# One chip core, three chained layers: TensorE's order fixed from the third group on, and another order of the start

## The chip, the core and the metric

The kernel runs on one NeuronCore of a Trainium2 chip, as one launch. The metric is device time in microseconds, the median of several executions. The core's engines work side by side, each through its own queue in order: TensorE (PE in the rows; PEld is its weight loads) multiplies matrices into PSUM, VectorE (DVE) and ScalarE (ACT) read PSUM and do elementwise work, GpSimd (POOL) does small jobs and indirect transfers, and SyncE (SP) issues the loads.

## The reference

Three layers follow each other on 4 x 768 = 3072 tokens of 384 numbers (8 heads of 48): a gated linear attention, a gated MLP with RMS norm, and a mixture of 8 experts with one expert per token.

```
for t in range(S):
    state = alpha[:, :, t, :, None] * state + np.einsum('bhd,bhe->bhde', k[:, :, t], v[:, :, t])
    y[:, :, t] = np.einsum('bhd,bhde->bhe', q[:, :, t], state)
...
xn = x / sqrt(mean(x*x) + 1e-6) * rms_g
x2 = (silu(xn @ w_gate) * (xn @ w_val)) @ w_out
...
e = argmax(x2 @ r_gate);  h = maximum(x2 @ w1[e], 0)
out = gate_w * sigmoid(x2 @ r_ogate)[e] * (h @ w2[e])
```

All inputs and outputs are 32-bit floats. The kernel splits each operand of the large products into a high and a low part and adds three products (high x high, high x low, low x high).

## The kernel before

**Tiles and groups.** The tokens are cut into 24 tiles of 128 tokens, numbered from 0; three tiles make a group of 384 tokens, and there are 8 groups. A tile's attention has a prework (alpha, q and k turned so that features lie on partitions, two scans along the tokens, two multiplies; `prework`, `prework_nat`) and five stages (`stages`): the score `ps_s` (line 416: 8 matmuls, two per head pair, that use rows 0 to 47 and 64 to 111 and write two banks), a transpose of the keys `ps_k` (L436), the output `ps_y` (L447 with the running state in the tile `wide`, L451 with the masked scores P), the new state `ps_st` (L472), and the transpose of the normed tile `ps_x` (L493). For tiles below `NAT` = 5 the prework turns the operands on TensorE from a buffer `nat` (L270); for tiles up to `PET` - 1 it does so from `row_a`, `row_k`, `row_q` (L371), three groups of four transposes per tile; from tile `PET` on, VectorE turns them (L376) out of block buffers `blk_a`, `blk_k`, `blk_q`, which take four loads each (L250).

**The MLP.** A group goes through 12 steps j, each of three slots: gate `ps_g` and value `ps_v` (9 matmuls each of 128 x 384, `mm3`, L595) and, one step later, the output `ps_o` (9 matmuls, `m_out`, L629). Between value and output stand a multiply on VectorE (`tt`, L606), a copy on ScalarE (`hh`, L609) and a subtraction on VectorE (`hl`, L615). The first two groups run in four pieces, s = 0 to 3 (groups 0 and 1 with the first six steps of the weights, then with the last six), since the weights arrive as 64-bit numbers and are converted on VectorE meanwhile (`conv_step`, L515 to L531). From s = 4 on (group 2), one piece is one group. `due` says in which slots the attention's stages of tiles 3 to 8 are written, a condition in the loop over g does the same for the later ones. Behind group 7 come the experts.

**The order.** The program is written in this order, and a scheduler then orders each engine's instructions by its own estimate of when each can start. `tc.keep_in_program_order(ins)` pins an instruction to the order of the source. Before the change, that is done for the warm-up matmuls (`warm`, L805, into the bank `junk`) and for instructions of VectorE, ScalarE and GpSimd whose kind stands in the list in force (`pace`; `K0` for the start, `K1` for s = 0, `K2` later). No attention or MLP matmul is pinned. The start, the attention of tiles 0 to 2 and the first loads, is written out by hand in two strings, `START` and `LOADS`: a, r, k, q are pieces of a tile's prework, s, n, y, d, x its stages, c three conversion steps, w6 six warm-up matmuls.

```python
def pace(kind, ins):
    if kind in paced[0] or kind.rstrip('0123456789') in paced[0]:
        tc.keep_in_program_order(ins)
```

Of the kernel before, what the change touches and what calls it, by code (L numbers as in the profile page):

```python
# [17 lines left out]
OFF = bass.IndirectOffsetOnAxis  # L18

CFG = {  # L20
    'START': 'a0 r0 c a1 w6 q0 k0 k1 r1 q1 w0 s0 s0 a2 y0 s1 r2 c q2 y0 w0 s1 x0 k2 y1 w4 y1 x1 s2 s2 y2 y2 x2 n1 n0 c n2 l l x2 d1 d0 c d2 w0 x0 x1 d2 d1 d0',
    'LOADS': 'a0 q0 a1 k0 q1 k1 a2 v0 w g k2 v1 q2 w w w r w v2 w w w w',
    'SEATS': (3, 5, 4, 6, 1, 1, 0, 5, 0, 2, 4, 4, 5, 3, 3, 2, 6, 1, 4, 4, 4, 2, 2, 1, 6, 3, 0, 6, 6, 4),
# [6 lines left out]
    'AHEAD': 0,  # L30
    'PREP6': 9,
    'CR': [3, 4, 3, 4],
    'PRN': [1, 2, 1, 2],
    'JS': 6,
    'ABUF': 1,
    'ZBUF': 1,
    'IB': 0,
    'RA0': 2,
    'RB0': 13,
    'XG': 3,  # L40
    'TS': 3,
    'RA': 7,
    'RB': 9,
    'LEADG': 6,
    'NAT': 5,
    'PET': 8,
    'NO': 'arkq',
}

# [3 lines left out]
def gla_glu_moe_kernel(  # L53
# [16 lines left out]
    nc = tc.nc  # L70
    P = 128
# [132 lines left out]
    xT = {}  # L204
    SEATS = CFG['SEATS']
    spread = [True]
    junk = [psM.tile([P, 4, P], F32, tag='o2', name='junk')]
    paced = [CFG['K0']]

# [191 lines left out]
    def stages(t):  # L401
        b, c = place_of[t]
        first, final = c == 0, c == NCH - 1
        en, qT, kT = pre[t]
        Sc = state_of[b % BS]
        S_ = wide[0]
        rs = [slice(64 * hh, 64 * hh + D) for hh in range(2)]
        g, ti = divmod(t, GT)
        Pt = {}

        def score():
            ps = [bank([P, NP, P], "ps_s") for _ in range(2)]
            for p in range(NP):
                for hh in range(2):
                    r = slice(64 * hh, 64 * hh + D)
                    nc.tensor.matmul(ps[hh][:, p, :], lhsT=kT[r, p, :], rhs=qT[r, p, :], start=True, stop=True)  # L416

            def post():
                if not first:
                    nc.vector.tensor_tensor(out=Sc, in0=Sc, in1=en.to_broadcast([P, NP, D]), op=ALU.mult)  # L420
                    for hh in range(2):
                        nc.scalar.activation(S_[rs[hh], :, hh * D:hh * D + D], Sc[rs[hh]], AF.Copy)
                mb = mask.to_broadcast([P, NP, P])
                for hh in range(2):
                    Ph = seat_of(t, f"P{hh}", [P, NP, P])
                    pace(f'Ph{t}', nc.vector.tensor_tensor(out=Ph, in0=ps[hh], in1=mb, op=ALU.mult))
                    Pt[hh] = Ph
            return post
        yield score

        def ktr():
            if final:
                return None
            ps = bank([P, NP, P], "ps_k")
            for p in range(NP):
                nc.tensor.transpose(ps[:, p, :], kT[:, p, :], ident)  # L436
            kn = seat_of(t, "kn", [P, H, 64])
            nc.scalar.activation(kn, ps.rearrange("p a (h d) -> p (a h) d", h=2), AF.Copy)
            Pt["kn"] = kn
            return None  # L440
        yield ktr

        def outp():
            ps = bank([P, DM], "ps_y")
            if not first:
                for p in range(NP):
                    nc.tensor.matmul(ps[:, p * 2 * D:p * 2 * D + 2 * D], lhsT=qT[:, p, :], rhs=S_[:, p, :],  # L447
                                     start=(p == 0), stop=False, skip_group_check=True)
            for h in (0, 2, 4, 6, 1, 3, 5, 7):
                for u in (slice(0, 64), slice(64, P)):  # L450
                    nc.tensor.matmul(ps[u, h * D:h * D + D], lhsT=Pt[h % 2][:, h // 2, u], rhs=vt[t][:, h, :],  # L451
                                     start=first, stop=True, skip_group_check=True)

            def post():
                xn = seat_of(t, "xn", [P, DM])
                ss = att.tile([P, 1], F32, tag="ss", name="ss", bufs=2)
                pace(f'xs{t}', nc.scalar.activation(xn, ps, AF.Square, accum_out=ss))  # L457
                nc.gpsimd.tensor_scalar(out=ss, in0=ss, scalar1=1.0 / DM, scalar2=1e-6, op0=ALU.mult, op1=ALU.add)  # L458
                pace(f'ss{t}', nc.gpsimd.tensor_tensor(out=ss, in0=ss, in1=mhalf, op=ALU.pow))
                pace(f'xa{t}', nc.scalar.activation(xn, ps, AF.Copy, scale=ss[:, 0:1]))  # L460
                Pt["xn"] = xn
            return post
        yield outp

        def state():
            if final:
                return None
            kn = Pt["kn"]
            ps = bank([P, NP, D], "ps_st")
            for p in range(NP):  # L470
                for hh in range(2):
                    nc.tensor.matmul(ps[64 * hh:64 * hh + 64, p, :], lhsT=kn[:, 2 * p + hh, :],  # L472
                                     rhs=vt[t][:, 2 * p + hh, :], start=True, stop=True)

            def post():
                if first:
                    nc.scalar.activation(Sc, ps, AF.Copy)
                else:
                    nc.vector.tensor_tensor(out=Sc, in0=ps, in1=Sc, op=ALU.add)
            return post  # L480
        yield state

        def xtr():
            if t and t + 2 < NTILE:
                load_v(t + 2)
            if ti == 0:
                xT[g] = (act.tile([P, KD, G], F32R, tag="xh", name="xh"),
                         act.tile([P, KD, G], F32R, tag="xl", name="xl"))
            xh, xl = xT[g]
            xn = Pt["xn"]  # L490
            ps = bank([P, KD, P], "ps_x")
            for kc in range(KD):
                nc.tensor.transpose(ps[:, kc, :], xn[:, kc * P:kc * P + P], ident)  # L493
            sl = slice(ti * P, ti * P + P)

            def post():
                xf = xn.rearrange("p (a b) -> p a b", a=KD)
                for kc in range(KD):
                    pace(f'xg{t}', nc.scalar.activation(xf[:, kc, :], ps[:, kc, :], AF.Copy, scale=gT[:, kc:kc + 1]))
                pace(f'xh{t}', nc.scalar.activation(xh[:, :, sl], xf, AF.Copy))  # L500
                pace(f'xl{t}', nc.vector.tensor_tensor(out=xl[:, :, sl], in0=xf, in1=f(xh[:, :, sl]), op=ALU.subtract))
            return post
        yield xtr
# [87 lines left out]
    def mm3(ps, wh, wl, xh, xl):  # L591
        n = 0
        for kc in range(KD):
            for a_, b_ in ((wh, xh), (wh, xl), (wl, xh)):
                nc.tensor.matmul(ps, lhsT=a_[:, kc, :], rhs=b_[:, kc, :],  # L595
                                 start=(n == 0), stop=(n == 3 * KD - 1))
                n += 1

    def m_val(g, j):
# [21 lines left out]
    def m_out(s, j):  # L621
# [4 lines left out]
        for i in range(GT):  # L626
            sl = slice(i * P, i * P + P)
            for n, (a_, b_) in enumerate(((hh, "woh"), (hh, "wol"), (hl, "woh"))):
                nc.tensor.matmul(obank[s][i], lhsT=a_[:, sl], rhs=weight(b_, j),  # L629
                                 start=(j == j0 and n == 0), stop=(j == j1 - 1 and n == 2))  # L630

    rows = {}

# [55 lines left out]
    def route_b(g):  # L689
        oh, ohb, ohc, m8, og, se = rt.pop(g)  # L690
        R = rows[g]
        ps = psR[0].tile([P, GT + 1, E], F32, tag=psR[1], name="ps_r")
        nc.tensor.matmul(ps[:, 0:1, :], lhsT=tri_b, rhs=ohb[:, 0:1, :], start=True, stop=True)
        for i in range(1, GT):
            nc.tensor.matmul(ps[:, i, :], lhsT=tri_b, rhs=ohb[:, i, :], start=True, stop=False)
            nc.tensor.matmul(ps[:, i, :], lhsT=ones_b, rhs=ohc[:, i - 1, :], start=False, stop=True)
        nc.tensor.matmul(ps[:, GT, :], lhsT=ones_b, rhs=ohc[:, GT - 1, :], start=True, stop=True)
        bc = [P, GT, E]

        nc.vector.tensor_scalar(out=se, in0=se, scalar1=1e-9, scalar2=2.0, op0=ALU.add, op1=ALU.mult)  # L700
# [151 lines left out]
    def due(s, n):  # L852
# [1 line left out]
        if s == 0:  # L854
            return done < GS and (n + 1 - AHEAD) * GS >= (done + 1) * (N - AHEAD - CFG['TS'])
        k_ = done - GS
        return (n + 1 + N * (s - 2)) * GS >= (k_ + 1) * 2 * N and k_ < GS and (k_ < NST - 1 or s >= CFG['XG'])

    for s in range(4):
        N = 3 * (runs[s][2] - runs[s][1])  # L860
        paced[0] = CFG['K2'] if s else CFG['K1']
        for n in range(N):
# [193 lines left out]

    for g in range(2, NG):
        last = g == NG - 1
        if last:
            psA.release()  # L1060
            att.release()
# [285 lines left out]
```

## Time and profile before

| | before |
|---|---|
| median of 3 runs | 876.1 us (875.66 to 876.71) |
| profiled execution | 880.26 us, span 878.6 us |
| TensorE busy | 856.1 us, 97% |
| VectorE / ScalarE / GpSimd busy | 489.3 / 326.0 / 143.8 us |
| chain that ended last | TensorE 85%, DMA 5%, issue 4% |
| mean granted TensorE clock | 0.99 |

Times in the profile are of one execution, which lies 4.2 us above the median; its span is counted from the first to the last instruction. Matmuls overlap, so their durations add up to more than the time they take: what one costs is read from one start to the next. A matmul of 32-bit floats (not of the kind fp32r that the wide ones use) shows as two rows, so a score of 8 shows as x16.

### The profile page before, as it was taken

What the parts mean: (1) busy time and instruction counts of PE and PEld (TensorE: products, weight loads), DVE (VectorE), ACT (ScalarE), POOL (GpSimd) and SP (SyncE); (2) the same over time, 40 slices, a digit from 0 to 9 for tenths busy, and PEclk for the clock granted to TensorE, in tenths of its full rate; (3) what the DMA queues carried; (4) which work ended last, traced back from release to release, by engine and by line L of the source; (5) the groups of instructions that cost most, each with busy time, mean ns of one, the idle gap of its engine ahead of it and who ended that gap; (6) DMA issues with size and microseconds to landing.
All of it is one profiled execution on the core that took longest, in us unless ns stands there. A gap on an engine that the chain in (4) does not pass through costs nothing.

```text
span 878.6 us, 15655 instructions
## 1 busy us (share of the span) xinstructions
PE 856.1 (97%) x6042; PEld 814.5 (93%) x6042; DVE 489.3 (56%) x1108; ACT 326.0 (37%) x708; POOL 143.8 (16%) x204
## 2 busy tenths in 40 slices
PE   7999999999999999999999999999999999999994
PEld 6799999899999999999999999999988999999994
DVE  7899987576854656655665552244454443444330
ACT  1655554234333233332322333334234442445431
POOL 2001001001100100010010010013032343344331
PEclk8999999999999999999999999999999999999998
DMA  9855534493311222132231010023056164256510
GB/s 190 181 163 149 175 83 122 117 258 89 104 49 36 78 57 61 43 87 60 59 87 47 13 37 1 1 93 98 1 182 197 60 212 144 65 190 198 178 41 24
DMA packets 121660, 88.46 MB, mean 101 GB/s; under 512 B 58219, under 2 KB 116716, under 8 KB 121584
## 3 DMA queue, kind: packets, MB, share of 16 engines
q1 hardware_dynamic: 117120, 77.97, 33.4%
q0 software_dynamic: 4464, 9.48, 3.1%
q8 instruction: 48, 0.79, 0.4%
q14 instruction: 28, 0.23, 0.1%
HBM read 71.62 MB, written 16.07 MB: 100 GB/s over the span
## 4 chain that ended last, share of the span: by engine, by line
PE 85%; DMA 5%; issue 4%; DVE 2%; POOL 1%; ACT 1%; SPq 1%; POOLq 0%; DVEq 0%; ACTq 0%
PE ps_o L629 18%; PE ps_v L595 18%; PE ps_g L595 18%; PE ps_b L1037 8%; PE ps_h L595 7%; PE ps_s L416 4%; PE ps_y L451 3%; DMA st<-in_moe_w_dram 3%; PE ps_y L447 2%; DMA er<-bucket 1%; PE ps_st L472 1%; PE ps_k L436 1%; PE ps_x L493 1%; POOL out_dram L1053 1%; PE pc L560 1%
## 5 line engine op out<-in xcount | busy, mean ns | idle before, releaser
L606 DVE TENSOR_TENSOR tt<-tt,ps_v 128x384 f32<-128x384 f32 x96 | 52.8, 550 | 140.9 <-PE ps_v L595 136.5
L587 ACT ACTIVATE tt<-ps_g 128x384 f32<-128x384 f32 x96 | 47.0, 490 | 135.4 <-PE ps_g L595 132.3
L609 ACT ACTIVATE hh<-tt 128x384 fp32r<-128x384 f32 x96 | 50.2, 523 | 119.6 <-DVE tt L606 119.2
L615 DVE TENSOR_TENSOR hl<-tt,hh 128x384 fp32r<-128x384 f32 x96 | 54.4, 567 | 28.1 <-ACT hh L609 27.4
L1037 PE MATMUL ps_b<-w2a,h 128*128 128x384 f32 (+2 forms) x336 | 67.4, 339 | 1.1 <-ACT h L1021 1.1
L595 PE MATMUL ps_g<-xh,wgh 128*128 128x384 f32 x192 | 68.1, 355 | 0.0
L595 PE MATMUL ps_v<-xh,wvh 128*128 128x384 f32 x192 | 68.0, 354 | 0.0
L1022 DVE SCALAR_TENSOR_TENSOR h<-ps_h,h 128x256 fp32r<-128x256 f32 (+6 forms) x72 | 38.0, 531 | 52.3 <-ACT h L1021 52.0
L629 PE MATMUL ps_o<-wol,hh 128*128 128x400 f32 x192 | 66.6, 347 | 0.0
L629 PE MATMUL ps_o<-woh,hh 128*128 128x400 f32 x192 | 66.5, 353 | 0.0
L1037 PE MATMUL ps_b<-w2b,h 128*114 128x384 f32 (+3 forms) x336 | 65.0, 338 | 0.2 <-ACT h L1021 0.2
L595 PE MATMUL ps_g<-xh,wgl 128*128 128x384 f32 x192 | 65.1, 339 | 0.0
L595 PE MATMUL ps_v<-xh,wvl 128*128 128x384 f32 x192 | 65.0, 339 | 0.0
L595 PE MATMUL ps_g<-xl,wgh 128*128 128x384 f32 x192 | 64.9, 338 | 0.0
L629 PE MATMUL ps_o<-woh,hl 128*128 128x400 f32 x192 | 64.7, 346 | 0.0
L595 PE MATMUL ps_v<-xl,wvh 128*128 128x384 f32 x192 | 64.7, 337 | 0.0
L1037 PEld LDWEIGHTS ps_b<-w2a,h 128*128 128x128 f32 (+2 forms) x336 | 57.5, 181 | 2.6 <-ACT h L1021 2.0
L1037 PEld LDWEIGHTS ps_b<-w2b,h 128*114 128x114 f32 (+3 forms) x336 | 57.5, 175 | 2.1 <-ACT h L1021 0.6
L595 PE MATMUL ps_h<-x,w1b 128*128 128x456 f32 (+3 forms) x288 | 58.5, 344 | 0.3 <-DVE h L1022 0.2
L1021 ACT ACTIVATE h<-ps_h 128x256 fp32r<-128x256 f32 (+6 forms) x72 | 33.3, 467 | 64.8 <-PE ps_h L595 60.4
L595 PE MATMUL ps_h<-x,w1a 128*128 128x256 f32 (+3 forms) x288 | 53.5, 328 | 0.6 <-DVE h L1022 0.6
L458 POOL TENSOR_SCALAR ss<-ss 128x1 f32<-128x1 f32 x24 | 6.4, 266 | 281.0 <-ACT xn L457 276.1
(284 smaller groups left out, 1994.9 us busy)
## 6 DMA issues: line engine op xcount, KB each, us to landing
st<-in_moe_w_dram SPq DMA_DIRECT2D x64, 384.0 KB, 5.4
bucket<-zero SPq DMA_DIRECT2D x8, 772.0 KB, 6.2
stg<-in_moe_w_gate_dram SPq DMA_DIRECT2D x12, 384.0 KB, 3.9
stg<-in_moe_w_val_dram SPq DMA_DIRECT2D x12, 384.0 KB, 3.7
stg<-in_moe_w_out_dram SPq DMA_DIRECT2D x12, 384.0 KB, 3.0
v<-in_v_dram SPq DMA_DIRECT2D x23, 192.0 KB, 2.8
blk_a<-in_alpha_dram SPq DMA_DIRECT2D x32, 96.0 KB, 2.2
blk_k<-in_k_dram SPq DMA_DIRECT2D x32, 96.0 KB, 2.3
```

The lines of the kernel that those rows point to most:

```text
L416: nc.tensor.matmul(ps[hh][:, p, :], lhsT=kT[r, p, :], rhs=qT[r, p, :], start=True, stop=True)
L447: nc.tensor.matmul(ps[:, p * 2 * D:p * 2 * D + 2 * D], lhsT=qT[:, p, :], rhs=S_[:, p, :], start=(p == 0), stop=False, skip_group_check=True)
L451: nc.tensor.matmul(ps[u, h * D:h * D + D], lhsT=Pt[h % 2][:, h // 2, u], rhs=vt[t][:, h, :], start=first, stop=True, skip_group_check=True)
L587: nc.scalar.activation(tt, ps, AF.Silu)
L595: nc.tensor.matmul(ps, lhsT=a_[:, kc, :], rhs=b_[:, kc, :], start=(n == 0), stop=(n == 3 * KD - 1))
L606: nc.vector.tensor_tensor(out=tt, in0=tt, in1=ps, op=ALU.mult)
L609: nc.scalar.activation(hh, tt, AF.Copy)
L615: nc.vector.tensor_tensor(out=hl, in0=tt, in1=f(hh), op=ALU.subtract)
L629: nc.tensor.matmul(obank[s][i], lhsT=a_[:, sl], rhs=weight(b_, j), start=(j == j0 and n == 0), stop=(j == j1 - 1 and n == 2))
L1021: nc.scalar.activation(hh[:, 0, :], ps, AF.Relu)
L1022: nc.vector.scalar_tensor_tensor(out=hh[:, 1, :], in0=ps, scalar=0.0, in1=f(hh[:, 0, :]), op0=ALU.max, op1=ALU.subtract)
L1037: ins = nc.tensor.matmul(ob2[u][i][0:r], lhsT=hh[:, a_, sl], rhs=we[p][b_][:, j, :], start=(j == 0 and m == 0), stop=(j == KF2 - 1 and m = ...
```

## The change

Every matmul and transpose of the attention, the MLP and the routing is handed to a new function `seq`, which pins it to the order of the source while `strict` is set. That is from piece s = `STRICT` = 4 on, which is group 2, up to group 6; the last group stays free.

The other edits: `PET` 8 to 7, so tile 7 is turned on VectorE. `XO` = 2 moves the stages of tiles 6 to 8 two slots ahead, and `XG` = 0 lets the last of them stand in the third piece. `START` has three more warm-ups (w3, w2, w1) and some pieces in another order; `LOADS` brings the third tile's v forward. `CR` and `PRN` change how many conversion and prework steps a slot writes, `PREP6` where tile 6's prework begins, `SEATS` one bank, `K0` to `K2` some pinned kinds. `LP` is an empty interval before and after.

```diff
-    'START': 'a0 r0 c a1 w6 q0 k0 k1 r1 q1 w0 s0 s0 a2 y0 s1 r2 c q2 y0 w0 s1 x0 k2 y1 w4 y1 x1 s2 s2 y2 y2 x2 n1 n0 c n2 l l x2 d1 d0 c d2 w0 x0 x1 d2 d1 d0',
+    'START': 'a0 r0 a1 w6 c q0 k0 k1 r1 q1 w0 s0 s0 a2 y0 s1 r2 c q2 y0 s1 k2 w0 y1 w4 x0 y1 x1 s2 s2 y2 y2 x2 n1 n0 c n2 l l x2 d1 w3 d1 d0 w2 c x0 d2 d2 x1 w1 d0',
...
-    'LP': (0, 0),
+    'LP': (20, 18),
...
-    'PREP6': 9,
-    'CR': [3, 4, 3, 4],
-    'PRN': [1, 2, 1, 2],
+    'PREP6': 7,
+    'CR': [2, 5, 3, 5],
+    'PRN': [1, 2, 0, 1],
...
-    'XG': 3,
+    'XG': 0,
...
-    'PET': 8,
+    'XO': 2,
+    'STRICT': 4,
+    'PET': 7,
...
+    strict = [False]
+
+    def seq(ins):
+
+        if strict[0]:
+            tc.keep_in_program_order(ins)
...
-                    nc.tensor.matmul(ps[hh][:, p, :], lhsT=kT[r, p, :], rhs=qT[r, p, :], start=True, stop=True)
+                    seq(nc.tensor.matmul(ps[hh][:, p, :], lhsT=kT[r, p, :], rhs=qT[r, p, :], start=True, stop=True))
...
-        return (n + 1 + N * (s - 2)) * GS >= (k_ + 1) * 2 * N and k_ < GS and (k_ < NST - 1 or s >= CFG['XG'])
+        return (n + 1 + CFG['XO'] + N * (s - 2)) * GS >= (k_ + 1) * 2 * N and k_ < GS and (k_ < NST - 1 or s >= CFG['XG'])
...
     for s in range(4):
+        strict[0] = s >= CFG['STRICT']
...
     for g in range(2, NG):
         last = g == NG - 1
+        strict[0] = g + 2 >= CFG['STRICT'] and not last
```

What stands where now, at three places. In the new file all lines from there on are 9 to 11 higher (the score is L425). The first place is TensorE's order around the score of tile 12, in group 3. Before:

```order
L595 MATMUL ps_g<-xh,wgle 128x384
L416 MATMUL ps_s<-qT,kT 128x128
L595 MATMUL ps_v<-xh,wvhe 128x384
...
L629 MATMUL ps_o<-wohe,hl 128x400
L416 MATMUL ps_s<-qT,kT 128x128 x7
L595 MATMUL ps_g<-xh,wghe 128x384
```

With the change:

```order
L638 MATMUL ps_o<-wole,hh 128x400
L638 MATMUL ps_o<-wohe,hl 128x400
L425 MATMUL ps_s<-qT,kT 128x128 x8
L604 MATMUL ps_g<-xh,wghe 128x384
L604 MATMUL ps_g<-xl,wghe 128x384
```

One of the eight score matmuls stood ahead of a value and an output product; now all eight stand together. Of tiles 10 to 23, 13 are cut in this way before, and none now.

The second place is TensorE's order in the start, behind the four warm-up matmuls that end the first two tiles' outputs (`side` is a place of tile 1 or 2, `kT` here tile 0's). Before:

```order
L270 MATMUL ps_n<-ident,nat 128x128 x4
L493 MATMUL ps_x<-ident,side 128x128 x3
L416 MATMUL ps_s<-side 128x128 x8
L436 MATMUL ps_k<-ident,kT 128x128 x8
L552 MATMUL pt<-ident,Fo 128x128 x3
L436 MATMUL ps_k<-ident,side 128x128 x4
L472 MATMUL ps_st<-v,side 64x48 x8
```

With the change:

```order
L425 MATMUL ps_s<-side 128x128 x8
L445 MATMUL ps_k<-ident,kT 128x128 x8
L502 MATMUL ps_x<-ident,side 128x128 x3
L445 MATMUL ps_k<-ident,side 128x128 x4
L481 MATMUL ps_st<-v,side 64x48 x8
L814 LDWEIGHTS ones_b
L814 MATMUL junk<-ones_b 128x512
...
L279 MATMUL ps_n<-ident,nat 128x128 x4
L561 MATMUL pt<-ident,Fo 128x128 x3
```

The four transposes ahead of the score have gone further up, into the outputs of tiles 0 and 1, the score of tile 2 stands first, and three warm-ups have come in; two and one more stand later.

The third place is TensorE's order at the score of tile 9, the first one under the fixed order, in the new program:

```order
L425 MATMUL ps_s<-qT,kT 128x128 x8
L604 MATMUL ps_v<-xh,wvh 128x384
...
L445 MATMUL ps_k<-ident,kT 128x128 x4
...
L456 MATMUL ps_y<-wide_125,qT 128x96 x4
L460 MATMUL ps_y<-v,P_2487 64x48 x8
```

Nine value matmuls and nine output matmuls are left out in the two gaps. For tiles 10 to 23 two more gate products and one more value product stand between the score and the output.

## Rows read from the trace of the kernel before

**Rows 1.** Page, part 1: busy time of each engine.
```profile
PE 856.1 (97%) x6042; PEld 814.5 (93%) x6042; DVE 489.3 (56%) x1108; ACT 326.0 (37%) x708; POOL 143.8 (16%) x204
```

**Rows 2.** Stages: length; busy PE, PEld, DVE, ACT, POOL (count); PEclk; DMA share, GB/s.
```profile
50.00:75.00 25.00, 25.00 (x216) 23.52 (x215) 24.14 (x57) 13.38 (x33) 1.27 (x3) 1.00 0.59 155
150.00:560.00 410.00, 410.00 (x3092) 387.27 (x3091) 234.41 (x562) 133.99 (x321) 33.55 (x67) 1.00 0.28 71
```

**Rows 3.** Timeline of TensorE, tile 12: start, duration, line, op, out<-in, count.
```profile
266.73 0.34 PE L595 MATMUL ps_g<-xl,wghe 128*128 128x384 f32 x1
266.90 0.34 PE L595 MATMUL ps_g<-xh,wgle 128*128 128x384 f32 x1
267.18 0.48 PE L416 MATMUL ps_s<-qT,kT 48*128 48x128 f32 x2
267.59 0.44 PE L595 MATMUL ps_v<-xh,wvhe 128*128 128x384 f32 x1
267.87 0.34 PE L595 MATMUL ps_v<-xl,wvhe 128*128 128x384 f32 x1
...
271.03 1.16 PE L416 MATMUL ps_s<-qT,kT 48*128 48x128 f32 x14
272.11 0.45 PE L595 MATMUL ps_g<-xh,wghe 128*128 128x384 f32 x1
```

**Rows 4.** Timeline of TensorE, tile 10, whose score is whole.
```profile
222.94 1.16 PE L416 MATMUL ps_s<-qT,kT 48*128 48x128 f32 x16
224.04 0.18 PE L693 MATMUL ps_r<-ohb,tri_b 128*128 128x8 bf16 x1
```

**Rows 5.** Timeline of TensorE, tile 13, score in 2 and 6.
```profile
291.90 0.49 PE L416 MATMUL ps_s<-qT,kT 48*128 48x128 f32 x4
...
295.76 0.94 PE L416 MATMUL ps_s<-qT,kT 48*128 48x128 f32 x12
296.63 0.45 PE L595 MATMUL ps_g<-xh,wgh 128*128 128x384 f32 x1
```

**Rows 6.** Timeline of TensorE, tile 18, first of two lone output pieces.
```profile
422.87 0.32 PE L451 MATMUL ps_y<-v,P 128*64 128x48 f32 x2
423.12 0.44 PE L595 MATMUL ps_g<-xh,wgh 128*128 128x384 f32 x1
```

**Rows 7.** Timeline of TensorE, tile 7: first and last of six score pieces.
```profile
152.38 0.48 PE L416 MATMUL ps_s<-qT,kT 48*128 48x128 f32 x2
...
166.62 0.48 PE L416 MATMUL ps_s<-qT,kT 48*128 48x128 f32 x2
```

**Rows 8.** Timeline of TensorE, tile 7: one of three groups of transposes.
```profile
140.24 0.60 PE L371 MATMUL ps_n<-ident,row_k 128*128 128x128 f32 x4
140.59 0.43 PE L629 MATMUL ps_o<-wol,hh 128*128 128x400 f32 x1
```

**Rows 9.** Groups by line: VectorE's transposes; busy time, mean ns, idle before.
```profile
L376 DVE STREAM_TRANSPOSE qT<-blk_q 128x512 f32<-128x512 f32 x16 | 17.6, 1100 | 0.3 <-PE ps_y L447 0.2
```

**Rows 10.** Timeline of TensorE: the first six warm-up matmuls.
```profile
7.49 1.67 PE L805 MATMUL junk<-ones_b 128*128 128x512 bf16 x6
```

**Rows 11.** Timeline of TensorE in the start: its two longest waits after 25 us.
```profile
29.84 0.66 PE L436 MATMUL ps_k<-ident,side 128*128 128x128 f32 x4 [0.87 <-ACT side L438]
...
35.42 0.63 PE L270 MATMUL ps_n<-ident,nat 128*128 128x128 f32 x4 [0.70 <-PE ps_n L270]
```

**Rows 12.** Timeline of VectorE in the start: its longest wait after 6 us.
```profile
25.71 0.69 DVE L340 TENSOR_TENSOR side<-ps_n,side 128x512 f32<-128x512 f32 x1 [1.84 <-PE ps_n L270]
```

**Rows 13.** Page, part 5: the masks.
```profile
L426 DVE TENSOR_TENSOR P<-ps_s,mask 128x512 f32<-128x512 f32 x46 | 29.9, 684 | 12.8 <-PE ps_s L416 12.8
```

**Rows 14.** Page, part 5: VectorE's multiply behind each value product.
```profile
L606 DVE TENSOR_TENSOR tt<-tt,ps_v 128x384 f32<-128x384 f32 x96 | 52.8, 550 | 140.9 <-PE ps_v L595 136.5
```

**Rows 15.** Page, part 6: zero fills and loads, KB each, us to landing.
```profile
bucket<-zero SPq DMA_DIRECT2D x8, 772.0 KB, 6.2
...
blk_a<-in_alpha_dram SPq DMA_DIRECT2D x32, 96.0 KB, 2.2
```

More of the change, by code (lines that the diff above doesn't have):

```diff
@@ L20 @@
 CFG = {
-    'START': 'a0 r0 c a1 w6 q0 k0 k1 r1 q1 w0 s0 s0 a2 y0 s1 r2 c q2 y0 w0 s1 x0 k2 y1 w4 y1 x1 s2 s2 y2 y2 x2 n1 n0 c n2 l l x2 d1 d0 c d2 w0 x0 x1 d2 d1 d0',
-    'LOADS': 'a0 q0 a1 k0 q1 k1 a2 v0 w g k2 v1 q2 w w w r w v2 w w w w',
-    'SEATS': (3, 5, 4, 6, 1, 1, 0, 5, 0, 2, 4, 4, 5, 3, 3, 2, 6, 1, 4, 4, 4, 2, 2, 1, 6, 3, 0, 6, 6, 4),
+    'START': 'a0 r0 a1 w6 c q0 k0 k1 r1 q1 w0 s0 s0 a2 y0 s1 r2 c q2 y0 s1 k2 w0 y1 w4 x0 y1 x1 s2 s2 y2 y2 x2 n1 n0 c n2 l l x2 d1 w3 d1 d0 w2 c x0 d2 d2 x1 w1 d0',
+    'LOADS': 'a0 q0 a1 k0 q1 k1 a2 v0 w g k2 v1 q2 w v2 w w r w w w w w',
+    'SEATS': (3, 5, 4, 6, 1, 1, 0, 5, 0, 2, 4, 4, 5, 0, 3, 2, 6, 1, 4, 4, 4, 2, 2, 1, 6, 3, 0, 6, 6, 4),
     'QM': 'vddddd',
     'SM': 'dad',
[4 rows of a table removed]
[4 rows of a table added]
     'AHEAD': 0,
-    'PREP6': 9,
-    'CR': [3, 4, 3, 4],
-    'PRN': [1, 2, 1, 2],
+    'PREP6': 7,
+    'CR': [2, 5, 3, 5],
+    'PRN': [1, 2, 0, 1],
     'JS': 6,
@@ L435, in ktr @@
             for p in range(NP):
-                nc.tensor.transpose(ps[:, p, :], kT[:, p, :], ident)
+                seq(nc.tensor.transpose(ps[:, p, :], kT[:, p, :], ident))
             kn = seat_of(t, "kn", [P, H, 64])
@@ L446, in outp @@
                 for p in range(NP):
-                    nc.tensor.matmul(ps[:, p * 2 * D:p * 2 * D + 2 * D], lhsT=qT[:, p, :], rhs=S_[:, p, :],
-                                     start=(p == 0), stop=False, skip_group_check=True)
+                    seq(nc.tensor.matmul(ps[:, p * 2 * D:p * 2 * D + 2 * D], lhsT=qT[:, p, :], rhs=S_[:, p, :],
+                                     start=(p == 0), stop=False, skip_group_check=True))
             for h in (0, 2, 4, 6, 1, 3, 5, 7):
                 for u in (slice(0, 64), slice(64, P)):
-                    nc.tensor.matmul(ps[u, h * D:h * D + D], lhsT=Pt[h % 2][:, h // 2, u], rhs=vt[t][:, h, :],
-                                     start=first, stop=True, skip_group_check=True)
+                    seq(nc.tensor.matmul(ps[u, h * D:h * D + D], lhsT=Pt[h % 2][:, h // 2, u], rhs=vt[t][:, h, :],
+                                     start=first, stop=True, skip_group_check=True))
             def post():
@@ L471, in state @@
                 for hh in range(2):
-                    nc.tensor.matmul(ps[64 * hh:64 * hh + 64, p, :], lhsT=kn[:, 2 * p + hh, :],
-                                     rhs=vt[t][:, 2 * p + hh, :], start=True, stop=True)
+                    seq(nc.tensor.matmul(ps[64 * hh:64 * hh + 64, p, :], lhsT=kn[:, 2 * p + hh, :],
+                                     rhs=vt[t][:, 2 * p + hh, :], start=True, stop=True))
             def post():
@@ L492, in xtr @@
             for kc in range(KD):
-                nc.tensor.transpose(ps[:, kc, :], xn[:, kc * P:kc * P + P], ident)
+                seq(nc.tensor.transpose(ps[:, kc, :], xn[:, kc * P:kc * P + P], ident))
             sl = slice(ti * P, ti * P + P)
@@ L594, in mm3 @@
             for a_, b_ in ((wh, xh), (wh, xl), (wl, xh)):
-                nc.tensor.matmul(ps, lhsT=a_[:, kc, :], rhs=b_[:, kc, :],
-                                 start=(n == 0), stop=(n == 3 * KD - 1))
+                seq(nc.tensor.matmul(ps, lhsT=a_[:, kc, :], rhs=b_[:, kc, :],
+                                 start=(n == 0), stop=(n == 3 * KD - 1)))
                 n += 1
@@ L628, in m_out @@
             for n, (a_, b_) in enumerate(((hh, "woh"), (hh, "wol"), (hl, "woh"))):
-                nc.tensor.matmul(obank[s][i], lhsT=a_[:, sl], rhs=weight(b_, j),
-                                 start=(j == j0 and n == 0), stop=(j == j1 - 1 and n == 2))
+                seq(nc.tensor.matmul(obank[s][i], lhsT=a_[:, sl], rhs=weight(b_, j),
+                                 start=(j == j0 and n == 0), stop=(j == j1 - 1 and n == 2)))
     rows = {}
@@ L692, in route_b @@
         ps = psR[0].tile([P, GT + 1, E], F32, tag=psR[1], name="ps_r")
-        nc.tensor.matmul(ps[:, 0:1, :], lhsT=tri_b, rhs=ohb[:, 0:1, :], start=True, stop=True)
+        seq(nc.tensor.matmul(ps[:, 0:1, :], lhsT=tri_b, rhs=ohb[:, 0:1, :], start=True, stop=True))
         for i in range(1, GT):
-            nc.tensor.matmul(ps[:, i, :], lhsT=tri_b, rhs=ohb[:, i, :], start=True, stop=False)
-            nc.tensor.matmul(ps[:, i, :], lhsT=ones_b, rhs=ohc[:, i - 1, :], start=False, stop=True)
-        nc.tensor.matmul(ps[:, GT, :], lhsT=ones_b, rhs=ohc[:, GT - 1, :], start=True, stop=True)
+            seq(nc.tensor.matmul(ps[:, i, :], lhsT=tri_b, rhs=ohb[:, i, :], start=True, stop=False))
+            seq(nc.tensor.matmul(ps[:, i, :], lhsT=ones_b, rhs=ohc[:, i - 1, :], start=False, stop=True))
+        seq(nc.tensor.matmul(ps[:, GT, :], lhsT=ones_b, rhs=ohc[:, GT - 1, :], start=True, stop=True))
         bc = [P, GT, E]
```

6 rows, old and new, of the table CFG are left out of this document.

## The prediction

> **What bounds the kernel now.** The first view is the page's busy times: TensorE is busy for 97% of the span, VectorE for 56% [rows 1]. The reader is to see that time can leave this kernel in two ways only: TensorE gets less to do, or its few idle microseconds go. The second view, busy time by stage, says where which holds. From 50 to 75 us TensorE is busy for 25.00 of 25 us, but VectorE, which converts the weights there, for 24.14 too; from 150 to 560 us TensorE has 410.00 of 410 us and VectorE 234.41, at a granted clock of 1.00 in both stretches [rows 2]. So from the third group on TensorE alone sets the pace, and whatever shortens its stream shortens the run; before 125 us VectorE stands close behind it.
>
> The third view, TensorE's instructions in order of time, shows what its stream pays for more than it must. Matmuls are pipelined, so I read prices as the distance from one start to the next, not as durations. Two wide matmuls start 0.17 us apart; the last one before a score is followed 0.28 us later, and the first one after it needs 0.28 us again: some 0.21 us for the two crossings together [rows 3]. The scores themselves are pairs that use 48 rows each and start together; a lone first score still holds TensorE for 0.41 us, and the seven left behind (14 halves in the trace) hold it for 1.08 us, against 1.10 us for all eight in one piece [rows 3, 4]. A score cut into 1 and 7 thus costs 0.41 + 0.21 - 0.02 = 0.60 us more than a whole one. Cut into 2 and 6, the first piece holds TensorE about as long (its duration is 0.49 us against 0.48), and the rest only 0.87 us [rows 5]: 0.41 + 0.21 - 0.23 = 0.39 us more.
>
> **The change part by part.** *The order of the source from the third group on.* In the order of before, 13 of the 14 tiles from 10 to 23 (numbered from 0) have their score cut: nine into 1 and 7, three into 2 and 6, and one into 1, 1 and 6. In the new order all are whole. 9 x 0.60 + 3 x 0.39 + (2 x 0.62 - 0.23 = 1.01) = 7.6 us. One output product is cut twice as well: two lone pieces start a wide matmul 0.25 us later each [rows 6]; with 0.21 for the two crossings apiece, less about 0.14 that the rest gets shorter, 0.8 us. The products with the wide state are cut in most tiles too, but they use all 128 rows, so I put no price on them. All this lies on TensorE while it has no idle time, so all of it counts: **-8.4 us**.
>
> The page TensorEngine Tiling (Array Packing) of the Trainium skill, section Tiling Modes, says that a change of tiling mode drains the engine. By that rule alone, which knows nothing of a pair that is torn apart, each of the 14 cuts would cost what a cut between two pairs costs, 0.39 us, and the scores would give 5.5 us instead of 7.6. The rows price the odd cut higher, and I take the rows.
>
> *Tiles 7 and 8, in the second half of the first two groups.* The score of tile 7 stands in six pieces of which the first and the last are shown [rows 7]; each holds TensorE for some 0.41 us and pays 0.21 for its crossings, 3.7 us in all. The new order has 1 and 7: 0.41 + 1.08 + 0.42 = 1.9. Tile 8 goes from two pieces to one (0.39), tile 4 from two runs of four to one run of eight (0.2 for a pair of crossings). **-2.4 us**.
>
> *One tile fewer is turned on TensorE (PET 8 to 7).* Three groups of four transposes go, 0.35 us each [rows 8] and 0.10 for the slower wide matmul behind: **-1.3 us**. They come back as three VectorE transposes of 1.10 us [rows 9] around 140 us, shortly before the stretch in which VectorE is busy for 57% of the time [rows 2]; 3.3 us there are covered by TensorE's matmuls, and would cost 3.3 us if they were not. ScalarE loses three copies, and three loads on SP's queue become twelve; that is the second rival.
>
> *The start.* Six warm-up matmuls are added between the first tiles; at the full clock six of them last 1.67 us [rows 10], at the lower level about twice that. They stand where TensorE waits anyway, 0.87 us for ScalarE and 0.70 us in its own queue [rows 11]. Against them, a group of transposes now comes earlier, which feeds the multiply that VectorE waited 1.84 us for [rows 12]. The chain through the third tile's output product to the first wide matmul is otherwise the same. I take **0**, and keep -1.8 (all of VectorE's wait goes through) and +1.7 (no cover) for the range.
>
> *Loads, conversions, pacing.* The order on SP, VectorE and ScalarE before 150 us changes a little; the amount does not, and the later conversions give VectorE slightly less to do in the first half-group. The cover is TensorE's full stream; if it is gone, VectorE's 24.14 of 25 us [rows 2] decides, which is the first rival.
>
> *New waits.* With its order fixed, TensorE can no longer run ahead of a piece that isn't ready. The tightest place is tile 9, the first in strict order: between its score and the products that need the masked scores stand only nine value matmuls, four transposes and nine output matmuls, 18 x 0.17 + 0.35 = 3.4 us. VectorE has two masks to do in that time, 0.68 us each [rows 13], behind what else is queued. Elsewhere three more blocks of nine lie between. VectorE has usually been idle when a value product ends: 136.5 us over 96 of them [rows 14], 1.4 us apiece, so there is room. I put **+1.0 us** on tile 9 and on the early stage together; the bounds are 0 and 3.
>
> The sum is -8.4 - 2.4 - 1.3 + 0 + 1.0 = **-11.1 us**. The profiled execution took 880.26 us, 4.2 us over the median of the three runs; the pieces are priced in it, and 0.5% of 11 us is nothing. Set against the median: 876.1 - 11.1 = **865.0 us**.
>
> **The rivals.**
> *The early gains are taken back by VectorE.* Until 125 us it is as full as TensorE [rows 2]. If it sets the pace there, or through the conversions that later slots wait for, the 3.7 us of tiles 4 to 8 and of the transposes come to nothing: 876.1 - 8.4 + 1.0 = 868.7 us. For it speaks 24.14 of 25; against it, most of those gains lie after 130 us, where VectorE has air.
>
> *Loads arrive late.* Tiles 7 to 9 are loaded in blocks on SP's queue among eight zero fills of 772 KB, 6.2 us each to land, and blocks need 2.2 us alone [rows 15]. The change puts one more tile of blocks there and leaves less time for it. One fill ahead of a block that the strict order needs costs about 6.2 us less the 1.0 already counted: 870.2 us. Against it: TensorE, with 410.00 of 410 us, waits for no load there before the change [rows 2].
>
> *Slower: the fixed order stalls in every tile.* If TensorE stands at its next matmul in each of the 15 tiles from 9 on, for the length of two masks (2 x 0.68 = 1.4 us [rows 13]) that VectorE had not finished, 15 x 1.4 = 21 us come on top: 886 us. From (11.1 / 15 =) 0.75 us a tile on, the change loses. For it: the scheduler moved pieces ahead for some reason. The page TensorE: Matmul & The Clock Gate, section Step-by-step, says that matmuls stay in program order and only weight loads are pulled ahead, so nothing would fill such a stall. Against it: VectorE's idle time before the value products [rows 14].
>
> *No change.* If the cuts filled time in which TensorE would have waited for the same data, whole scores only move the wait: 876 us. TensorE's busy time alone cannot tell the two apart. Against it: the cut piece has its price wherever it stands [rows 3], and VectorE is idle for 43% of that stretch [rows 2].
>
> **How the numbers follow.** The forecast gets 0.55, the early gains lost 0.19, late loads 0.13, no change 0.06, slower 0.07. The forecast's own span is 861.5 to 867.5: the start's -1.8 and no new waits on one side, 2 us more of waits on the other. With the first two rivals the range is **861 to 870.5 us**; the last two stay out. A measurement of this kernel tells about 0.2%, 1.8 us, from no change. Faster by more: 0.55 + 0.19 + 0.13 = 0.87; within: 0.06; slower: 0.07.
>
> **What would show it.** Right: after 205 us every score is one row of 16 halves, 1.1 us; TensorE stays busy without a gap from 150 to 560 us; the distance from the first wide matmul of the third group to the first expert matmul shrinks by some 8 us, that from the first wide matmul to the third group by 2 to 4; the first wide matmul starts within 2 us of where it did. The forecast is wrong if TensorE shows idle time before the value products or masked products after 200 us (slower), idle time with a block load as releaser from 150 to 210 us (loads), or if the stage up to 130 us is as long as before (VectorE).

## The result, and the profile after

| | before | after |
|---|---|---|
| median | 876.4 us (875.66 to 878.18, 4 runs) | 868.15 us (865.15 to 868.93, 4 runs) |
| ratio | | 0.9892, 95% interval 0.9864 to 0.9919 |
| span of the profiled execution | 878.6 us | 863.4 us |
| TensorE busy | 856.1 us | 840.6 us |

The kernel became faster, by 8.3 us between the medians and by 7 to 12 us by the interval. The profiled spans lie 15.2 us apart, which is more: the profiled execution of before (880.26 us) lies 3.9 us over this median, and that of the changed kernel (865.15 us) 3.0 us under its own. The part of it that belongs to the profile of before is told under the start, below.

The page of the changed kernel, part 1, answers to [rows 1]; TensorE has almost as many rows (6036 for 6042), and its busy time is 15.5 us shorter:

```profile
PE 840.6 (97%) x6036; PEld 806.6 (93%) x6036; DVE 491.0 (57%) x1111; ACT 324.7 (38%) x705; POOL 142.2 (16%) x204
```

The same two stages as in [rows 2] (length; busy PE, PEld, DVE, ACT, POOL with counts; granted clock; DMA share; GB/s):

```profile
50.00:75.00 25.00, 24.77 (x233) 23.01 (x232) 23.05 (x52) 14.05 (x36) 1.12 (x3) 1.00 0.56 150
150.00:560.00 410.00, 410.00 (x3146) 395.31 (x3146) 241.79 (x582) 137.99 (x325) 32.52 (x67) 1.00 0.26 67
```

From 150 to 560 us TensorE still has no gap, and passes 54 more rows in the same 410 us (3146 for 3092): time went because the stream got shorter, not because a wait went. TensorE's timeline at the score of tile 12, where [rows 3] showed one piece of 2 rows and one of 14:

```profile
263.00 0.34 PE L638 MATMUL ps_o<-wohe,hl 128*128 128x400 f32 x1
263.27 1.16 PE L425 MATMUL ps_s<-qT,kT 48*128 48x128 f32 x16
264.36 0.45 PE L604 MATMUL ps_g<-xh,wghe 128*128 128x384 f32 x1
```

One row of 16 halves, 1.09 us to the next start, as forecast; it is the same for all tiles from 8 to 23. Tile 7, in six pieces before [rows 7], has two, 1 and 7:

```profile
146.54 0.48 PE L425 MATMUL ps_s<-qT,kT 48*128 48x128 f32 x2
...
148.72 1.16 PE L425 MATMUL ps_s<-qT,kT 48*128 48x128 f32 x14
```

What is new is a wait, the longest of TensorE between 40 and 610 us. The forecast had +1.0 us of new waits for tile 9 and the early stage together; this one alone is longer. TensorE, then VectorE (the wait in brackets, with what ended it), then SP's queue:

```profile
116.68 0.45 PE L604 MATMUL ps_v<-xh,wvh 128*128 128x384 f32 x1 [1.89 <-DVE tt L615]
```

```profile
113.28 1.10 DVE L385 STREAM_TRANSPOSE qT<-blk_q 128x512 f32<-128x512 f32 x1 [2.90 <-DMA blk_q<-in_q_dram]
114.23 1.07 DVE L385 STREAM_TRANSPOSE kT<-blk_k 128x512 f32<-128x512 f32 x1
...
116.07 0.55 DVE L615 TENSOR_TENSOR tt<-tt,ps_v 128x384 f32<-128x384 f32 x1
```

```profile
105.44 0.86 SPq L259 DMA_DIRECT2D blk_q<-in_q_dram  x2
106.39 0.38 SPq L519 DMA_DIRECT2D stg<-in_moe_w_out_dram  x1
106.83 0.90 SPq L259 DMA_DIRECT2D blk_q<-in_q_dram  x2
```

Tile 7 is now turned on VectorE. Its block loads stand among the last weight loads (`stg`); those of q and k land some 5 us after they are issued. The transposes wait for them with the multiply `tt` behind them in VectorE's queue, and TensorE's next value product waits for `tt`. This is the rival "loads arrive late" in a mild form, earlier than it was expected and behind weight loads instead of zero fills. A second small loss lies in the last group: two expert loads land late, ScalarE stands at them (1.84 and 2.18 us) with `hh` behind, TensorE waits for `hh`, and the first half of group 7 takes 30.0 us instead of 29.0 (ScalarE, then TensorE):

```profile
579.09 0.85 ACT L963 ACTIVATE w1a<-st 128x768 fp32r<-128x768 f32 x1 [2.18 <-DMA st<-in_moe_w_dram]
579.84 0.50 ACT L618 ACTIVATE hh<-tt 128x384 fp32r<-128x384 f32 x1
```

```profile
580.40 0.45 PE L638 MATMUL ps_o<-woh,hh 128*128 128x400 f32 x1 [0.42 <-ACT hh L618]
```

### The profile page after: what moved, and what is told of

The parts are those of the page before. It is cut to its first block, busy times and chain, and to the rows that moved or that the text cites. A ratio compares the mean times of both kernels' runs of the same rounds, so it can differ in the third digit from the quotient of the medians.

```text
span 863.4 us, 15649 instructions
## 1 busy us (share of the span) xinstructions
PE 840.6 (97%) x6036; PEld 806.6 (93%) x6036; DVE 491.0 (57%) x1111; ACT 324.7 (38%) x705; POOL 142.2 (16%) x204
## 4 chain that ended last, share of the span: by engine, by line
PE 79%; DVE 7%; issue 5%; DMA 4%; POOL 2%; SPq 1%; ACT 1%; POOLq 0%; DVEq 0%; ACTq 0%
PE ps_o L638 17%; PE ps_v L604 16%; PE ps_g L604 16%; PE ps_b L1047 9%; PE ps_h L604 9%; PE ps_s L425 3%; DMA st<-in_moe_w_dram 3%; PE ps_y L460 2%; PE ps_y L456 2%; PE ps_st L481 1%; SPq L915 1%; PE ps_k L445 1%; PE ps_x L502 1%; PE ps_t L1011 1%; POOL out_dram L1063 1%
## 5 line engine op out<-in xcount | busy, mean ns | idle before, releaser
L615 DVE TENSOR_TENSOR tt<-tt,ps_v 128x384 f32<-128x384 f32 x96 | 52.9, 551 | 119.8 <-PE ps_v L604 116.8
```

What stands on the lines that cost most here:

```text
L615: nc.vector.tensor_tensor(out=tt, in0=tt, in1=ps, op=ALU.mult)
```

## The experiments

Three marks in TensorE's timeline cut every profile into stretches: the first wide matmul, the first wide matmul of the third group, the first expert matmul. Between the first and the last mark the starts of different executions play no part. The mark of the third group does not stand at the same work in every kernel, since the stages of tile 9 move across it. The fifth column therefore gives a part of the stretch before it, from the first wide matmul of the fourth group to that of the last: every kernel has the same scores, outputs and wide matmuls between these two marks. (Times are in us; the last group is the one with the number 7.)

| profile of | first wide at | to 3rd group | 3rd group to experts | of it, 4th to last group | first wide to experts | median, ratio to before |
|---|---|---|---|---|---|---|
| before | 38.77 | 166.3 | 420.5 | 290.1 | 586.8 | |
| XO, XG alone | 38.71 | 161.5 | 423.4 | 290.1 | 584.9 | 875.12, 0.9969 |
| fixed order alone | 35.76 | 164.7 | 415.7 | 282.8 | 580.4 | 871.31, 0.9935 |
| fixed order, XO, XG | 35.62 | 160.6 | 415.2 | 282.8 | 575.8 | 865.72, 0.9870 |
| all but the fixed order | 34.6 | 162.7 | 424.4 | 290.1 | 587.0 | 877.27, 1.0012 |
| after (all) | 34.28 | 160.9 | 416.2 | 282.8 | 577.2 | 868.15, 0.9892 |

**The fixed order alone**, in the kernel before:

```diff
+    'XO': 0,
+    'STRICT': 4,
...
+        strict[0] = g + 2 >= CFG['STRICT'] and not last
```

> The numbers of before with the fixed order from the third group on as the only change. Theory A (the cut scores in groups 2 to 6 carry the gain): TensorE's time from the first wide matmul to the first expert matmul falls by 7.5 to 9 us, the run by as much, to 867.5 to 869 us, a ratio of 0.990 to 0.9915. Theory B (the gain came from the start, whose first wide matmul stands 4.5 us earlier in the trace of the change): within 1.5 us of before, 875 us or more.

Measured: 871.31 us, ratio 0.9935 (0.9922 to 0.9948), a gain of 5.6 us (6.4 between the first wide and the first expert matmul), and less than expected. From the third group on every score is whole and the stretch falls to 415.7 us, but at its first matmul there is a wait that before did not have (TensorE, then ScalarE):

```profile
200.48 0.44 PE L604 MATMUL ps_g<-xh,wgh 128*128 128x384 f32 x1 [1.59 <-ACT xh L509]
```

```profile
198.99 0.88 ACT L508 ACTIVATE xn<-ps_x,gT 128x128 f32<-128x128 f32 x3 [0.85 <-PE ps_x L502]
199.90 0.52 ACT L509 ACTIVATE xh<-xn 128x384 fp32r<-128x384 f32 x1
```

The normed tile is turned late, and in the fixed order nothing may be put ahead of the gate product that needs it.

**All edits but the fixed order:**

```diff
-    'STRICT': 4,
+    'STRICT': 99,
```

> The changed kernel with the fixed order switched off and all its other numbers kept. Theory A: most of the cuts come back; 5 to 8 us slower than the change, 873 to 876 us. Theory B: as the change, 866 to 869 us.

Measured: 877.27 us, ratio 1.0012 (0.9994 to 1.003): no gain, where a few microseconds were expected. The cuts are all back: 28 score pieces for tiles 10 to 23, as before the change, instead of 14. The wait at 117 us is there too (2.07 us), and group 7 takes 1.2 us longer than before. With the other edits in place the fixed order is thus worth 424.4 - 416.2 = 8.2 us from the third group on. By the time, 877.27 us lies over the ranges of both theories; by the mechanism, theory A holds.

**XO and XG alone**, in the kernel before (`n + 3` is XO 2 written out):

```diff
-    'XG': 3,
+    'XG': 0,
...
-        return (n + 1 + N * (s - 2)) * GS >= (k_ + 1) * 2 * N and k_ < GS and (k_ < NST - 1 or s >= CFG['XG'])
+        return (n + 3 + N * (s - 2)) * GS >= (k_ + 1) * 2 * N and k_ < GS and (k_ < NST - 1 or s >= CFG['XG'])
```

> The kernel before with XO 2 and XG 0 alone, no fixed order and no other edit. Theory A (two gains that add up: the stages of tiles 6 to 8 two slots earlier cut fewer scores, 43 pieces in the TensorE order instead of 46 with fewer of them before group 2, and the fixed order gives 8.4 us): 1.5 to 3.5 us under before, 873.4 to 875.4 us; with the 865.7 us of both together the fixed order is then worth 8 to 9 us, and the 5.6 us it gave alone were that less the wait at the boundary. Theory B (the two earlier slots only help where the order is fixed, because all they do is remove that wait): within 1 us of before, 876 to 878 us.

**Fixed order with XO and XG**, no other edit:

```diff
-    'XG': 3,
+    'XG': 0,
...
-    'XO': 0,
+    'XO': 2,
```

> The kernel before with the fixed order and with XO 2 and XG 0, no other edit. Theory A (the fixed order alone lost 1.6 us at the boundary of the second and third group, where the first wide matmul of group 2 waited for ScalarE's copy of the normed tile; writing the stages two slots earlier removes that): the wait at 200 us falls from 1.59 to under 0.3 us, the distance from the third group to the first expert matmul stays at 415.5 to 416.5 us, the median is 869.2 to 870.3 us, 1.6 us under the run with the fixed order alone (871.3). Theory B (XO only shifts work from one piece to another): the median stays at 870.8 to 871.8 us.

Measured: XO and XG alone 875.12 us, ratio 0.9969 (0.9955 to 0.9983), 2.1 us under before; with the fixed order 865.72 us, ratio 0.9870 (0.9848 to 0.9892). Tile 7's six score pieces become one, which the two earlier slots do and not the fixed order. The wait at the boundary is gone; the same place as above, with nothing in brackets:

```profile
196.02 0.34 PE L638 MATMUL ps_o<-wohe,hl 128*128 128x400 f32 x1
196.20 0.34 PE L604 MATMUL ps_g<-xh,wgh 128*128 128x384 f32 x1
```

So the two edits do two things: they have a gain of their own, 2 us, as theory A of the run without the fixed order had it, and they take away the wait of 1.59 us that only the fixed order brings. The run with both was expected at 869.2 us or more and is 3.5 us faster, since its expectation counted the wait alone. On top of XO the fixed order gives 423.4 - 415.2 = 8.2 us from the third group on, the same number as between the other pair; the ratios give 8.7 us here and 10.5 us for the other pair. These two edits reach what all of them reach together: the start, the loads, the pacing and PET give nothing that the medians show.

**The start of before**, and **no added warm-ups**, each in the changed kernel. The first puts the old string `START` back; of the second the end of the string is shown:

```diff
-l l x2 d1 w3 d1 d0 w2 c x0 d2 d2 x1 w1 d0
+l l x2 d1 d1 d0 c x0 d2 d2 x1 d0
```

> The changed kernel with the start of before (its order of the first three tiles' pieces and none of the six added warm-ups). Theory A: the start is worth within 1.5 us either way, 866.5 to 870 us. Theory B: the start's 4.5 us are lost, 871 to 874 us, and the first wide matmul stands near 38.8 us again.

> The changed kernel without its six added warm-up matmuls, the rest of the start kept. If the six lie in TensorE's waits, as the prediction has it, nothing changes, 867 to 869 us; if they lie on the path, up to 1.7 us faster, 866.5 us; if they keep the granted clock up, the clock falls to 0.5 for a stretch before the first wide matmul and the run is 2 us or more slower, 870 us or more.

Measured: 868.32 us (0.9898, 0.9882 to 0.9914) and 866.16 us (0.9878, 0.9863 to 0.9892). The old start costs nothing in the median. Without the warm-ups the time is 2 us lower, although the granted clock fell to 0.80 and 0.86 between 30 and 40 us of its profile; but its interval and that of the changed kernel overlap.

**Tile 7 on TensorE again**, and the same without the warm-ups:

```diff
-    'PET': 7,
+    'PET': 8,
```

> The changed kernel with tile 7 turned on TensorE again (PET 8). Theory A (the prediction's -1.3 us for three groups of transposes is eaten by a wait for tile 7's block loads): TensorE's wait of 1.89 us near 117 us, where it stands for VectorE's product behind a VectorE transpose that waits for a block load, is gone (under 0.3 us), 1.3 us of transposes come back, so the median lies within 0.7 us of the changed kernel, 867.5 to 868.9 us, ratio to before 0.989. Theory B (the wait comes from the other pacing of the conversions, five steps in one slot): the wait stays above 1 us, and the transposes come on top: 869.5 us or more. Prediction's own view (the transposes were covered): 869.4 us and no wait to remove.

> The changed kernel with PET 8 and without its six added warm-up matmuls: both edits that seem to give nothing are undone. If the two act apart (warm-ups cost 2 us, PET nothing), 865.5 to 866.9 us, ratio to before 0.988. If the 2 us of the run without warm-ups came only from another granted clock or from chance, 867.5 to 869 us.

Measured: 872.56 us (0.9946, 0.9929 to 0.9963) and 872.03 us (0.9936, 0.9911 to 0.996). No expectation held: 872.56 us lies in the range of theory B, but the wait near 117 us, which theory B kept, is gone, and a longer one has come elsewhere; 872.03 us lies over both of its ranges. SP's queue, VectorE and TensorE with PET 8:

```profile
172.23 4.66 SPq L728 DMA_DIRECT2D bucket<-zero  x4
176.99 3.67 SPq L259 DMA_DIRECT2D blk_a<-in_alpha_dram  x4
```

```profile
191.90 1.08 DVE L385 STREAM_TRANSPOSE aT<-blk_a 128x512 f32<-128x512 f32 x1 [6.88 <-DMA blk_a<-in_alpha_dram]
```

```profile
197.02 0.69 PE L604 MATMUL ps_v<-xh,wvhe 128*128 128x384 f32 x1 [5.43 <-DVE tt L615]
197.51 0.52 PE L604 MATMUL ps_v<-xl,wvhe 128*128 128x384 f32 x1
```

A block load stands behind four zero fills, and TensorE pays 5.43 us for it. The two matmuls behind the wait last 0.69 and 0.52 us, against 0.45 and 0.34 elsewhere; the granted clock stands at the lower level:

```profile
190.00:195.00 5.00, 1.59 (x11) 1.32 (x9) 2.93 (x7) 0.00 (x0) 0.00 (x0) 0.93 0.51 116
195.00:200.00 5.00, 2.98 (x9) 2.98 (x10) 2.73 (x6) 2.20 (x6) 0.00 (x0) 0.50 0.51 110
200.00:205.00 5.00, 5.00 (x36) 4.62 (x35) 1.58 (x3) 1.01 (x2) 0.00 (x0) 0.88 0.00 0
```

The way to the third group takes 167.7 us, against 160.6 in the kernel with the fixed order, XO and XG, which has PET 8 too and none of this wait. So it is one or more of the other edits (start, loads, pinned kinds, pacing) that make PET 8 dear; which was not taken apart. With them, PET 7 is worth 4.4 us between the medians; without them it was not tried.

**The pacing of before** (CR, PRN, PREP6), then **only CR** and **only PREP6** as before:

```diff
-    'PREP6': 7,
-    'CR': [2, 5, 3, 5],
-    'PRN': [1, 2, 0, 1],
+    'PREP6': 9,
+    'CR': [3, 4, 3, 4],
+    'PRN': [1, 2, 1, 2],
```

> The changed kernel with the pacing of conversions and prework of before (CR, PRN, PREP6). Theory A (the wait near 117 us is for the block load of tile 7): with PET at 7 the block loads are still needed, and the wait on VectorE's product stays, above 1 us, somewhere between 100 and 125 us; median 867.5 to 869.5 us. Theory B (the wait comes from the pacing): the wait is gone, and the median falls by 1.5 us or more, to 866.6 us or less.

> The changed kernel with only the pacing of the conversions as before (CR 3, 4, 3, 4); PRN and PREP6 stay as changed. Tile 7's first block load then stands behind 34 weight loads on SP's queue instead of 31 (36 with all three undone). Theory A (the conversions' pace decides): the wait near 117 us is under 0.3 us, and the median 863.5 to 865.5 us as with all three undone. Theory B (tile 6's and 7's prework is written too early by PREP6 and its block loads still stand among the weight loads): a wait of 1 us or more behind a block load stays between 100 and 130 us, and the median is 866.5 to 868.5 us.

> The changed kernel with only PREP6 back at 9; CR and PRN stay as changed. The first block load stands behind 32 weight loads, and weight loads still stand among the blocks. Theory A (the conversions' pace decides): the wait stays, 1 us or more, and the median is 867 to 869 us. Theory B (PREP6 decides): the wait is gone, 864 to 866 us.

Measured: 863.97 us (0.9851, 0.9828 to 0.9874), 865.35 us (0.9854, 0.9828 to 0.9879) and 864.86 us (0.9851, 0.9825 to 0.9877). With all three undone, tile 7's first block load is issued at 113.86 us instead of 101.66, behind the weight loads, and TensorE waits for no load between 100 and 125 us, so my first theory of this run (the wait stays) is wrong. The way from the first wide to the first expert matmul is 574.9 us, 2.2 less than in the changed kernel, and the first half of group 7 is back at 29.0 us. With CR alone undone the wait is 0.98 us long and stands at 123 us behind the same transpose, between its two theories, with the median of the first; with PREP6 alone it is 1.36 us at 117 us, as expected for the case that the conversions decide, but the median is 2 us lower than expected there. CR and PREP6 each move the block loads, and neither alone takes the wait away; PRN alone was not tried. The median does not follow the wait here, so what the wait costs is read from the traces only. The profiles with PREP6 undone and after have the same span (863.6 and 863.4 us), while the medians lie 3.3 us apart. The other three executions of the changed kernel have no profile; their spans are 866.1 to 867.2 us at mean granted clocks of 0.989 to 0.994. The clock alone does not account for it, as the kernel with PREP6 undone has a span of 862.7 us at 0.994: why they are slower stays open.

**The pacing of before, and no added warm-ups:**

> The changed kernel with CR, PRN and PREP6 of before and without the six added warm-up matmuls. If the warm-ups cost what the first run without them showed (2 us), 861.5 to 862.8 us. If that difference was chance, or comes back as a wait for the third tile's data at the first wide matmul, as it did in the run with PET 8 and no warm-ups (1.45 us for v's load), 863.3 to 865 us.

Measured: 871.64 us (0.9926, 0.9905 to 0.9947), 7.7 us over the same kernel with the warm-ups (6.6 by the ratios), and outside both expectations. TensorE at the first wide matmuls, and two stages in the columns of the windows above:

```profile
36.61 0.44 PE L604 MATMUL ps_g<-xh,wgh 128*128 128x384 f32 x1 [1.41 <-ACT xh L509]
...
38.85 0.69 PE L604 MATMUL ps_g<-xl,wgh 128*128 128x384 f32 x1 [1.63 <-DVE xl L510]
```

```profile
35.00:40.00 5.00, 1.96 (x8) 1.44 (x7) 5.00 (x16) 3.37 (x7) 0.00 (x0) 0.79 1.08 289
40.00:45.00 5.00, 5.00 (x20) 4.90 (x19) 4.86 (x12) 1.60 (x4) 0.00 (x0) 0.53 0.49 153
```

With the warm-ups, the same two stages:

```profile
35.00:40.00 5.00, 5.00 (x30) 4.67 (x31) 5.00 (x15) 2.90 (x5) 0.00 (x0) 1.00 0.98 248
40.00:45.00 5.00, 5.00 (x60) 4.58 (x59) 5.00 (x11) 3.27 (x8) 0.00 (x0) 1.00 0.61 190
```

TensorE passes 28 rows in these 10 us instead of 90. Two things go together here: the scheduler, without the warm-ups, puts VectorE's `xl` and ScalarE's `xh` later, and behind the waits the clock falls. Which of them costs how much was not taken apart.

## Why the prediction was right

The measured 868.15 us lies 3.2 us over the forecast of 865.0, and outside the forecast's own span of 861.5 to 867.5. (By its own terms, -1.8 for the start and none of the 1.0 us of waits, that span would begin at 862.2.) It lies inside the range only because of the rivals, and 0.6 us from the first rival's 868.7. That nearness is luck: the rival let VectorE take back all early gains, and the trace shows the gain of the early scores in full and a load behind the largest loss.

**The fixed order (-8.4).** Right in mechanism and size: 8.2 us in two independent pairs of kernels, in the stretch from the third group to the experts. The strictest test is the column from the fourth group to the last. The prices of the prediction give 7 x 0.60 + 3 x 0.39 + 1.01 + 0.8 = 7.2 us for the tiles whose scores lie there (13 to 23), and every kernel with the fixed order takes 282.8 us where every one without takes 290.1, 7.3 us less. The scores' own share, from start to start, falls from 16.1 to 12.0 us, and the rest goes mainly at the crossings. The products with the wide state, which had no price, need none: whole, they hold TensorE some 1.5 us longer than cut (10.5 and 9.0 us), and the 15 crossings that go with their cuts give back about 1.3 us. The Trainium skill, page TensorEngine Tiling (Array Packing), section Tiling Modes, says that a change of tiling mode drains the engine. An estimate that takes this as one price for every cut, the 0.39 us of a cut between two pairs, gives 5.5 us for this column instead of 7.2; the trace stands with the rows' price for the odd pair.

**The early scores (-2.4).** Right in size: 2.1 us in the median and 1.9 in the trace (586.8 to 584.9), and XO and XG alone give it. The tiles that give it are in part others: in that kernel tile 7 is whole, tile 8 is still cut, and tile 9 is cut for the first time.

**New waits (+1.0, bounds 0 to 3).** The 2.9 us in the trace lie within the bounds, near their upper end; the place is not the one named. Nothing waits at tile 9, which I called the tightest place. The fixed order does bring a wait of 1.59 us, one stage earlier, at the first gate product of the third group; XO removes it, so that it shows only in the kernel with the fixed order alone. In its place stand 1.89 us at 117 us and 1.0 us in group 7.

**Transposes to VectorE (-1.3).** The step that failed is "3.3 us there are covered by TensorE's matmuls". Nothing shows that the VectorE work itself is not covered, as its idle time before `tt` is long (116.8 us in all, 136.5 before [rows 14]); what is not covered is the data of the transposes, the twelve loads that replace three. I had counted them and put them into a rival, but looked for the collision among the zero fills, and for the transposes around 140 us instead of at 113. In the trace the wait of 1.89 us is more than the 1.3 us that were to be gained.

**The start (0).** In the profiles the first wide matmul comes 4.5 us earlier, more than the 2 us that I allowed. Of that, 3.1 us are the profile of before itself: the same start gives 38.71 us in one execution and 35.62 in another (the last section). The edits give 35.62 - 34.28 = 1.3 us, inside the bounds, and the medians show none of it. That the warm-ups cost nothing was too simple: removing them moves other work too, for 2 us less (within the uncertainty) or 7.7 us more, depending on the pacing.

**The signs.** Every score is whole and TensorE has no gap from 150 to 560 us, as said. The two distances did not come out as said: the way to the third group shrinks by 5.4 us instead of 2 to 4, and that from there to the experts by 4.3 instead of some 8, because the mark between them moved. At the mark of the fourth group, which does not move against the scores, the parts are 3.4 us less from the first wide matmul to it, 7.3 less from it to the last group, and 1.1 more in the last group.

**The sum.** Between the first wide and the first expert matmul the traces differ by 586.8 - 577.2 = 9.6 us. The fixed order (8.2) and the early scores (1.9), less the two new waits (1.9 and 1.0), make 7.2 of it; the other 2.4 belong to the transposes that went, 1.3 by the forecast, and to the remaining edits, and no run takes them apart. With 1.3 us for the start the traces give 10.9 us; the ratio gives 9.5 us (876.4 x 0.0108) and the medians 8.3, where 11.1 was forecast. The traces thus agree with the forecast better than the medians do, and the one of the changed kernel is its fastest execution of four. The fixed order and XO without the other edits have 0.9870; the lowest ratio here, 0.9851, belongs to the changed kernel with the pacing of before and to that with PREP6 alone undone.

## What to carry to other kernels

Where TensorE has no gaps, price a cut operation from start to start, piece by piece: here the cuts of the scores cost in sum what their pieces' prices, 0.39 to 0.60 us a cut, came to, the cuts of the product with the wide state about nothing, and pinning the order of the source was worth the sum of the cuts. The same pin turned the first late operand into a wait, which writing its producer two slots earlier in the same edit removed. Work that goes to an idle engine must be costed with its loads: ask which loads stand ahead of them on the queue, and what stands behind the waiting instruction. Of a table of numbers tuned together, undo single entries only to learn a mechanism: what PET or the warm-ups were worth depended on the rest of the table.

## What the runs showed that I had not expected

The granted clock of the first 25 us differs between executions, and the time with it, by 3 us. In three of the fourteen profiles (before, XO and XG alone, only CR undone) TensorE waited 0.46 to 0.63 us near 10.2 us for the same load, with the clock at 1.00 (2.4 GHz), and from 15 to 25 us the clock was 0.50 or 0.51 (1.2 GHz); in a fourth, with the old start, it was 0.66 from 20 to 25 us, without that wait. Before, TensorE and two windows:

```profile
10.22 0.96 PE L270 MATMUL ps_n<-ident,nat 128*128 128x128 f32 x7 [0.63 <-DMA nat<-in_k_dram]
```

```profile
15.00:20.00 5.00, 5.00 (x52) 4.46 (x53) 4.03 (x11) 1.57 (x4) 0.76 (x2) 0.50 1.19 286
20.00:25.00 5.00, 5.00 (x42) 3.48 (x38) 3.87 (x9) 1.89 (x7) 0.75 (x2) 0.50 0.95 170
```

After, the same six warm-ups as in [rows 10] take 2.52 us instead of 1.67, the transposes follow without a wait, and the clock stays at 1.00:

```profile
7.40 2.52 PE L814 MATMUL junk<-ones_b 128*128 128x512 bf16 x6
9.76 1.47 PE L279 MATMUL ps_n<-ident,nat 128*128 128x128 f32 x12
```

```profile
15.00:20.00 5.00, 4.75 (x70) 3.83 (x68) 5.00 (x12) 1.60 (x4) 1.05 (x2) 1.00 1.16 285
```

Pairs with nearly the same start show the price: 38.71 and 35.62 us to the first wide matmul (XO and XG without and with the fixed order, which touches nothing there), 37.65 and 34.84 (CR undone, all three undone). That is 3.1 of the 4.2 us by which the profiled execution of before lay over its median. The other executions of that kernel, run again beside the experiments, show the same split: 13 with a mean granted clock of 0.988 to 0.991 took 878.8 to 880.8 us, and of 32 with 0.994 to 0.996 all but five took 876.0 to 877.6 us. So a few microseconds between two profiles of this kernel say nothing until the clock of the start is read. That the half microsecond of waiting makes the clock fall was not tested; it goes with it in all three.
